# Wider TensorE groups for shared expert slots and for attention's values and sums

## The chip, the cores and the metric

The kernel runs on one NeuronCore of one Trainium2 chip. The metric is the device time of one execution in microseconds; the kernel before took 1078.47 us (median of three runs, 1077.15 to 1081.84).

## The reference

Three stages follow one another, all in float32:

- attention over 4 batches, 12 heads, 448 positions, head size 64, with capped scores: `scores = cap * tanh(q k^T / 8 / cap)`, softmax, times `v`;
- a feed-forward layer on the 1792 tokens of 768 numbers: `h = x @ w_in` (768 x 2048), `g = h * clip(h + 3, 0, 6) / 6`, `g @ w_out` (2048 x 768);
- a mixture of 8 experts: each token goes to the expert with the largest logit; `relu(x @ w1[e]) @ w2[e]` (768 x 1024 and 1024 x 768), scaled by the gate's probability and by a sigmoid.

```python
scores = cap * np.tanh(scale * np.matmul(q, k.transpose(0, 1, 3, 2)) / cap)
attn = np.exp(scores - scores.max(-1, keepdims=True))
x = np.matmul(attn / (attn.sum(-1, keepdims=True) + 1e-09), v)
for e in range(E):
    mask = e_idx == e
    out[mask] = gate_w[mask, None] * eom[mask, e, None] * (np.maximum(x[mask] @ w1[e], 0.0) @ w2[e])
```

## The kernel before, in words

All work is entered into one list of operations (`work.add`) with an engine, a due time in ns, an estimated duration, the operations it waits for and the buffers it uses. A planner (`Work.run`, L94) then walks through time by its own estimates and, on each engine, issues the ready operation with the earliest due time. The result is a fixed program order for each engine; on the chip an engine works through that order and waits where something isn't there yet. An operation with the engine `pe` may hold several matmuls; these stay together in TensorE's order, and matmuls of other operations come only between operations. The engine `sp` stands for SyncE, which issues the weight loads. For a load the planner counts 1400 ns, then the bytes at a fixed rate on one common line for all loads, then 1100 ns.

Buffers come in rings. A ring hands out its tiles in turn (`take`), and every operation that uses a tile waits for all operations on the tile's previous holder. The order of `take` in the program thus sets who gets a PSUM bank after whom.

**Attention** works on pairs of heads (`pair`, L505), six pairs to a batch. From the second batch on it lies between feed-forward work of the batch before. A pair's scores are four blocks of 112 keys: matmuls into S (L527), tanh (L536) and exp (L540) on ScalarE, with the exponentials `ee` kept in a ring of seven tiles, and VectorE's running sum `es` (L548). Then `pv(c0)` (L555) multiplies the exponentials of two blocks with the values, for two heads in two column halves of the array, into bank U, and `total()` (L562) adds `es` over the partitions into bank T with a matrix of ones. These are plain float32 matmuls, and each appears as two instructions in the profile. The loop at L567 makes two TensorE operations of it: `pv(0)`, waiting for the first two exponentials, and `(pv(2), total())`, waiting for the other two and for the sum. After that the sums are turned into reciprocals and multiplied in (L587 to L599).

**Feed-forward and expert products** are full-width matmuls on `float32r`: each float32 factor is split into a high and a low part and three matmuls (`mm3`, L605 to L608) add up one product.

**Expert slots.** A main slot takes 128 tokens of one expert (`first`, `second`, `h_T`, `x_T`); its matmuls are the L606 to L608 rows with `xTm` and `hTm`. Each product works through 6 or 8 chunks of 128 weight rows, and the products of all slots run in one fixed order: `first(i)`, `second(i-1)`, `first(i+1)` and so on. Each product needs its transposed left side, which goes through banks T and U in the order of program text.

Two **shared slots** (`quad_x`, `quad_h`, `quad_y`) take the remainders of several experts: 128 columns in parts of 64, 32 and 32, one expert for each part. `quad_product` (L1394) makes such a product, first with w1 (6 chunks, 2 x 512 columns), then with w2 (8 chunks, 2 x 384 columns). For each chunk t and each column half c there is a load of three conditional transfers, one for each part, into a buffer of the ring `QB` (two buffers cut from the tile `spare`), and one TensorE operation of four 32-column matmuls (L1416, eight instructions in the profile) that is due at `at + (2t+c) per` and ends that half's use of the buffer:

```python
x = work.add("sp", due - 14e3, 400, load, [qr] + gone, [hb], NQ * w * 512)
...
last[c] = work.add("pe", due, 40 + 1.75 * w, mm, [x, last[c]] + ready, [hd, accs[c], hb])
```

The shared slots are entered after main slots 2, 4, 7 and 9, 11, 13 (`QI`, L1445), so their transposes (L1433) stand in the order for T and U behind those of these slots. `spare` was the feed-forward's buffer before (`YT`, `ROWS`, `lt`); the shared slots may load into it once the last batch's rows are stored (`gone`).

Of the kernel before, what the change touches and what calls it, by code (L numbers as in the profile page):

```python
# [9 lines left out]
F32 = mybir.dt.float32  # L10
# [171 lines left out]
def attention_ffn_moe(  # L182
# [16 lines left out]
    B, H, S, D = q.shape  # L199
# [3 lines left out]
    C = 4  # L203
    P = S // C
    KD = DM // 128
    KF = DFF // 128
    KE = DE // 128
# [6 lines left out]
    NQ = len(PARTS)  # L214
# [14 lines left out]
    def pool(name, **kw):  # L229
        g = tc.tile_pool(name=name, reuse_waits="tile", **kw)  # L230
        return g, g.__enter__()

    def close(*gs):
# [18 lines left out]
        out=tri, in_=tri, pattern=[[1, P]], compare_op=ALU.is_gt, fill=0.0, base=0, channel_multiplier=-1  # L252
# [30 lines left out]
    g_fa, ffa = pool("ffa", bufs=1, side="left")  # L283
# [4 lines left out]
    def copier(out, in_):  # L288
        def fn(eng):
            if eng == "dve":  # L290
                nc.vector.tensor_copy(out=out, in_=in_)
            else:
                nc.scalar.activation(out=out, in_=in_, func=ACTF.Copy)  # L293

        return fn
# [7 lines left out]
    for nm in ("S0", "S1"):  # L303
        t = psp.tile([128, 2, 512], F32, name=nm)
# [22 lines left out]
    RR = ring(ffb, 2, [128, S], "r")  # L327
    GT = ring(ffb, HF, [128, 2, S], "gT", F32R)
    nspare = KD * S + C * RW + S
    spare = ffa.tile([128, max(nspare, 2 * NQ * 512 + KE * 128)], F32, name="spare")  # L330
    YT = Ring([spare[:, d * S:(d + 1) * S] for d in range(KD)])
    ROWS = Ring([spare[:P, KD * S:KD * S + C * RW]])
    lt = spare[:, nspare - S:nspare]
# [5 lines left out]
    work = Work()  # L339
# [5 lines left out]
    def t_head(g):  # L345
        return g * T0 / H if g < H else T0 + (g - H) * T1 / H
# [158 lines left out]
    def pair(n):  # L505
        b, p = divmod(n, H // 2)
        t0, per = t_head(2 * n), (t_head(2 * n + 2) - t_head(2 * n)) / 2
        hv, lv = loaded[n, "v2"]
        hw, ready = turned_qk[n]
        w = hw.t  # L510
# [3 lines left out]
        hu, hsum = UR.take(), ES.take()  # L514
        uv, es = hu.t, hsum.t
        many = 1 if b == 0 else 2
        et, last = [], None
        for c0 in range(0, C, many):
            at = t0 + c0 * per / 2
# [12 lines left out]
            for c, h in enumerate(hs):  # L532
                sv = h.t[:P, :, 0:S]
                x = work.add(
                    "act", at - 4e3 + c * 2e3, 900,
                    lambda sv=sv: A.activation(out=sv, in_=sv, func=ACTF.Tanh, scale=rcap[:P]), [s] + caps, [h])  # L536
                he = EE.take()
                x = work.add(
                    "act", at - 3e3 + c * 2e3, 900,
                    lambda sv=sv, he=he: A.activation(out=he.t, in_=sv, func=ACTF.Exp, scale=capt[:P]), [x], [h, he])  # L540
                et.append((he, x))
                k = len(et) - 1
                if k == 0:
                    continue
                one = et[0][0] if k == 1 else hsum
                last = work.add(
                    "dve", at - 2e3 + c * 2e3, 1002,
                    lambda he=he, one=one: V.tensor_tensor(out=es, in0=one.t, in1=he.t, op=ALU.add),  # L548
                    [et[0][1], x, last], [he, one, hsum] if k == 1 else [he, hsum])


        hd = TR.take()
        dv = hd.t

        def pv(c0):  # L555
            for c in range(c0, c0 + 2):
                for r in range(2):
                    nc.tensor.matmul(  # L558
                        out=uv[64 * r:64 * r + 64, 0:S], lhsT=by_head(hv)[:, r, c], rhs=et[c][0].t[:, r],
                        start=(c == 0), stop=(c == C - 1))  # L560

        def total():  # L562
            for r in range(2):
                nc.tensor.matmul(out=dv[64 * r:64 * r + 64, 0:S], lhsT=ones[:, 0:64], rhs=es[:, r], start=True, stop=True)  # L564

        x = None
        for c0 in range(0, C, 2):  # L567
            hes = [et[c][0] for c in (c0, c0 + 1)]
            if c0 + 2 < C:
                x = work.add(  # L570
                    "pe", t0 + c0 * per / 2, 1700, lambda: pv(0), [et[0][1], et[1][1], lv], [hu, hv] + hes, rows=P)
            else:
                x = work.add(
                    "pe", t0 + c0 * per / 2, 2450, lambda c0=c0: (pv(c0), total()), [x, et[2][1], et[3][1], last],
                    [hu, hv, hd, hsum] + hes, rows=P)
# [6 lines left out]
        def blocks(t):  # L582
            return t.rearrange("p (n w) -> p n w", w=32)

        at = min(t0 + 2.5 * per, T0 + b * T1 - 6e3 + p * 500)
        pe = x
        x = work.add("act", at, 467, lambda: A.activation(out=us, in_=dv[:, 0:S], func=ACTF.Copy), [pe], [hd, hy])  # L587
        x = work.add("dve", at, 535, lambda: V.transpose(out=blocks(rt), in_=blocks(us)), [x], [hy, hr])
        x = work.add("dve", at, 160, lambda: V.reciprocal(out=rc, in_=blocks(rt)[:, :, 0:1]), [x], [hr, hc])
        x = work.add(  # L590
            "dve", at, 535, lambda: V.transpose(out=blocks(us), in_=rc.to_broadcast([128, nb, 32])), [x], [hc, hy])
        x = work.add(
            "dve", at, 535, lambda: V.tensor_tensor(out=ux, in0=uv[:, 0:S], in1=us, op=ALU.mult), [x, pe], [hu, hx, hy])
        x = work.add(("dve", "act"), at, (302, 467), copier(x2[:, 0], ux), [x], [hx, xt])
        x = work.add(
            "dve", at, 535,
            lambda: V.tensor_tensor(out=x2[:, 1], in0=ux, in1=x2[:, 0].bitcast(F32), op=ALU.subtract),
            [x], [hx, xt])
# [126 lines left out]
    def chain(at, ops, fn, after, use=()):  # L725

        steps = [None]

        def some(n):
            if steps[0] is None:  # L730
                steps[0] = fn()
            for _ in range(n):
                next(steps[0])

        def rest(n):
            some(n)
            assert next(steps[0], None) is None

        for j, n in enumerate(ops):
            fn_ = rest if j == len(ops) - 1 else some  # L740
            after = [work.add("dve", at + j * 1.9e3, 200 * n - 130, lambda n=n, fn_=fn_: fn_(n), after, use)]
        return after[0]
# [483 lines left out]
    et = chain(te, (5, 5, 5, 2), early_table, [sw, placed[B - 2]])  # L1226
    er = work.add("sp", te + 3e3, 200, lambda: registers("e", NEARLY, "eei"), [et])
    he, x = lists("e", NEARLY, te + 4e3, [et, listed[B - 2]], TU)
# [133 lines left out]
    hd_, x = lists("d", NDYN, tm + SOON + 13e3, [ltab, listed[B - 1]], F)  # L1362
# [1 line left out]
    lr = work.add("sp", tm + SOON + 14e3, 1000, lambda: registers("d", NDYN, "dei"), [ltab])  # L1364


    QB = Ring([spare[:, j * NQ * 512:(j + 1) * NQ * 512].rearrange("p (q w) -> p q w", q=NQ) for j in range(2)])
    QT = Ring([spare[:, 2 * NQ * 512:2 * NQ * 512 + KE * 128].rearrange("p (t n) -> p t n", n=128)])
    quad = []

    def quad_regs():
# [6 lines left out]
    hq_, x = lists("q", NG, tm + SOON + 18e3, [qtab, listed[B - 1]], F)  # L1378
    qpg = small([128, NSH, NQ], "qpages")
    x = work.add(  # L1380
        "dve", tm + SOON + 18e3, 70,
        lambda: V.tensor_copy(out=qpg.rearrange("p s j -> p (s j)"), in_=hq_.t[:, 0:NG]), [x], [hq_])
# [6 lines left out]
    x = work.add("pe", tm + SOON + 18e3, 400, joined, [x], [hs_])  # L1389
    qlist = work.add("dve", tm + SOON + 18e3, 70, lambda: numbers("q", hs_, NSH), [x], [hs_])  # L1390
    qr = work.add("sp", tm + SOON + 22e3, 1600, quad_regs, [qtab])
    gone = [fin[B - 1, C - 1], listed[B - 1]]

    def quad_product(s, hd, ready, many, src, w, at, per):  # L1394
        accs = [F.take() for _ in range(2)]
        last = [None, None]
        for t in range(many):
            for c in range(2):
                hb = QB.take()
                due = at + (2 * t + c) * per  # L1400

                def load(t=t, c=c, hb=hb):
                    for j, (e, some) in enumerate(quad[s * NQ:(s + 1) * NQ]):
                        nc.sync.dma_start(
                            out=hb.t[:, j, 0:w],
                            in_=src[bass.ds(e, 1)].rearrange("o a b -> (o a) b")[
                                t * 128:(t + 1) * 128, c * w:(c + 1) * w],
                            cond=some > 0, bounds_check="skip_entire_dma")

                x = work.add("sp", due - 14e3, 400, load, [qr] + gone, [hb], NQ * w * 512)  # L1410

                def mm(t=t, c=c, hb=hb, acc=accs[c].t):
                    for j, (o, n) in enumerate(PARTS):
                        for a in range(o, o + n, QW):
                            part = slice(a, a + QW)
                            nc.tensor.matmul(  # L1416
                                out=acc[part, 0:w], lhsT=hd.t[:, t, part], rhs=hb.t[:, j, 0:w],
                                start=(t == 0), stop=(t == many - 1))

                last[c] = work.add("pe", due, 40 + 1.75 * w, mm, [x, last[c]] + ready, [hd, accs[c], hb])  # L1420
        return list(zip(accs, last))

    def quad_turned(src, after, n, at):
        hd = QT.take()
        hk = n // 2
# [77 lines left out]
    for i in range(NMAIN, NS):  # L1503
        with tc.If(used > slots[i][1]):
            work = Work()
# [39 lines left out]
```

## Time and profile before

| | us |
|---|---|
| median of 3 runs | 1078.47 |
| profiled execution | 1078.56 |
| span of its trace | 1076.8 |
| TensorE busy (matmul) | 1037.4 (96%) |
| VectorE busy | 729.5 (68%) |
| ScalarE busy | 663.1 (62%) |
| GpSimd busy | 94.8 (9%) |
| chain that ended last: TensorE | 77% of the span |
| chain that ended last: DMA | 4% of the span |

How to read it: the span runs from the first to the last instruction of the trace, and the execution's time has 1.76 us around it. Busy time of TensorE is modelled for overlapping matmuls, so a stretch of close starts counts as full. In timeline rows the first number is the start, the second the time to the end of the last instruction in the row, `xN` the number of instructions merged, and a bracket the idle time before the row and what ended it. Rows merge neighbours of the same kind, so a row `x16` of L1416 is two operations side by side.

### The profile page before, as it was taken

How to read it: one execution, taken by the hardware profiler on the slowest of the kernel's cores; microseconds unless marked ns; L12 is line 12 of the kernel's file. 1: busy time of each engine (PE TensorE's matmuls, PEld its weight loads, DVE VectorE, ACT ScalarE, POOL GpSimd, SP SyncE). 2: the span in 40 equal slices, each digit the busy share in tenths (PEclk: the TensorE clock that was granted, in tenths of full speed). 3: DMA queues.
4: the chain of work that ended last, by engine and by line, in shares of the span. 5: the costliest groups of instructions: out<-in, count | busy, mean ns of one | idle time of the engine just before them, and what ended most of it. 6: DMA issues, size and time to landing. Idle time of an engine off the chain costs nothing.

```text
span 1076.8 us, 17039 instructions
## 1 busy us (share of the span) xinstructions
PE 1037.4 (96%) x5764; PEld 792.6 (74%) x5764; DVE 729.5 (68%) x1155; ACT 663.1 (62%) x916; POOL 94.8 (9%) x122
## 2 busy tenths in 40 slices
PE   6979999999999999999999999999899999999996
PEld 4436777776777777677787899998677776877773
DVE  5999988965754665774465582627977777777762
ACT  5987677744754754564674352527566776776762
POOL 3211112100000000000000100000211111111001
PEclk9999999999999999999999999999999999999999
DMA  9889799862243343253232284462387689857455
GB/s 268 237 244 284 244 287 296 275 201 76 84 145 90 104 124 85 70 164 101 59 114 64 66 310 152 132 234 89 113 287 237 227 291 369 314 206 282 142 175 158
DMA packets 113997, 199.24 MB, mean 185 GB/s; under 512 B 43578, under 2 KB 68026, under 8 KB 113344
## 3 DMA queue, kind: packets, MB, share of 16 engines
q1 hardware_dynamic: 104304, 161.90, 46.7%
q0 software_dynamic: 9600, 36.19, 10.8%
q8 instruction: 47, 0.77, 0.3%
q14 instruction: 46, 0.38, 0.1%
HBM read 224.19 MB, written 25.76 MB: 232 GB/s over the span
## 4 chain that ended last, share of the span: by engine, by line
PE 77%; issue 9%; DVE 6%; DMA 4%; ACT 1%; POOL 0%; SPq 0%; POOLq 0%; DVEq 0%
PE F L606 14%; PE F L608 13%; PE F L607 13%; PE U L558 6%; PE S L606 6%; PE S L527 5%; PE S L607 5%; PE S L608 5%; PE F L1416 2%; DMA out_dram<-y,tkd 2%; DMA spare<-in_moe_w_dram 2%; PE T L564 1%; DVE ring L1270 1%; PE T L489 1%; DVE es L548 1%
## 5 line engine op out<-in xcount | busy, mean ns | idle before, releaser
L635 DVE TENSOR_TENSOR ws<-wr,ws 128x768 fp32r<-128x768 f32 (+1 forms) x112 | 119.6, 1068 | 77.5 <-ACT ws L632 75.1
L632 ACT ACTIVATE ws<-wr 128x768 fp32r<-128x768 f32 (+1 forms) x112 | 104.6, 934 | 42.6 <-PE F L607 27.8
L606 PE MATMUL F<-gT,ws 128*128 128x448 f32 x320 | 121.5, 380 | 0.0
L608 PE MATMUL F<-gT,ws 128*128 128x448 f32 x320 | 117.0, 366 | 0.0
L607 PE MATMUL F<-gT,ws 128*128 128x448 f32 x320 | 116.9, 365 | 0.0
L536 ACT ACTIVATE S<-S,rcap 112x896 f32<-112x896 f32 x96 | 91.1, 980 | 24.2 <-PE S L527 23.8
L540 ACT ACTIVATE ee<-S,capt 112x896 f32<-112x896 f32 x96 | 93.3, 1016 | 0.2
L527 PE MATMUL S<-qk 64*112 64x448 f32 x576 | 76.6, 390 | 12.0 <-ACT qk L495 5.1
L606 PE MATMUL S<-ring,hTm 128*128 128x384 f32 x224 | 82.8, 370 | 0.0
L659 ACT ACTIVATE r<-F,three 128x448 f32<-128x448 f32 x64 | 40.7, 636 | 63.3 <-PE F L608 62.6
L607 PE MATMUL S<-ring,hTm 128*128 128x384 f32 x224 | 75.7, 338 | 1.4 <-DVE ring L1270 1.4
L527 PEld LDWEIGHTS S<-qk 64*112 64x112 f32 x576 | 47.2, 175 | 40.3 <-issue 13.6
L606 PEld LDWEIGHTS F<-gT,ws 128*128 128x128 f32 x320 | 60.1, 188 | 22.3 <-issue 18.2
L608 PE MATMUL S<-ring,hTm 128*128 128x384 f32 x224 | 75.7, 338 | 0.2 <-DVE hTm L1298 0.2
L606 PE MATMUL F<-xTa,ws 128*128 128x448 f32 x192 | 73.8, 384 | 1.6 <-ACT spare L293 0.9
L606 PE MATMUL F<-xTb,ws 128*128 128x448 f32 x192 | 73.7, 384 | 1.6 <-ACT spare L293 0.9
L558 PE MATMUL U<-ee,v 112*64 112x448 f32 x336 | 73.8, 561 | 0.0
L1270 DVE TENSOR_TENSOR ring<-w2B,ring 128x768 fp32r<-128x768 f32 x56 | 53.1, 958 | 30.2 <-ACT ring L1266 29.5
L607 PE MATMUL F<-xTb,ws 128*128 128x448 f32 x192 | 70.3, 366 | 0.0
L608 PE MATMUL F<-xTb,ws 128*128 128x448 f32 x192 | 70.2, 366 | 0.0
L1270 DVE TENSOR_TENSOR ring<-w2A,ring 128x768 fp32r<-128x768 f32 x56 | 53.0, 956 | 25.1 <-ACT ring L1266 21.8
L608 PE MATMUL F<-xTa,ws 128*128 128x448 f32 x192 | 69.8, 364 | 0.0
(291 smaller groups left out, 2287.3 us busy)
## 6 DMA issues: line engine op xcount, KB each, us to landing
wr<-wsi SPq DMA_DIRECT2D x64, 384.0 KB
wr<-wso SPq DMA_DIRECT2D x48, 512.0 KB
w1A<-in_moe_w_dram SPq DMA_DIRECT2D x42, 512.0 KB
w2A<-in_moe_w_dram SPq DMA_DIRECT2D x56, 384.0 KB
w1B<-in_moe_w_dram SPq DMA_DIRECT2D x42, 512.0 KB
w2B<-in_moe_w_dram SPq DMA_DIRECT2D x56, 384.0 KB
spare<-in_moe_w_dram SPq DMA_DIRECT2D x72, 256.0 KB
spare<-in_moe_w_dram SPq DMA_DIRECT2D x96, 192.0 KB
```

The source lines that it names most:

```text
L527: nc.tensor.matmul(out=h.t[:P, r, 0:S], lhsT=w[o, 1, i, (c0 + c) * P:(c0 + c + 1) * P], rhs=w[o, 0, j], start=(t == 0), stop=(t == 2))
L536: lambda sv=sv: A.activation(out=sv, in_=sv, func=ACTF.Tanh, scale=rcap[:P]), [s] + caps, [h])
L540: lambda sv=sv, he=he: A.activation(out=he.t, in_=sv, func=ACTF.Exp, scale=capt[:P]), [x], [h, he])
L558: nc.tensor.matmul(out=uv[64 * r:64 * r + 64, 0:S], lhsT=by_head(hv)[:, r, c], rhs=et[c][0].t[:, r], start=(c == 0), stop=(c == C - 1))
L606: nc.tensor.matmul(out=acc, lhsT=lh, rhs=rh, start=first, stop=False)
L607: nc.tensor.matmul(out=acc, lhsT=lh, rhs=rl, start=False, stop=False)
L608: nc.tensor.matmul(out=acc, lhsT=ll, rhs=rh, start=False, stop=last)
L632: lambda: A.activation(out=s[:, 0, 0:n], in_=t, func=ACTF.Copy), [x], [hw, hs])
L635: lambda: V.tensor_tensor(out=s[:, 1, 0:n], in0=t, in1=s[:, 0, 0:n].bitcast(F32), op=ALU.subtract),
L659: "act", t1, 518, lambda: A.activation(out=r, in_=acc, func=ACTF.Relu, bias=three), [last], [ha, hr])
L1270: lambda: V.tensor_tensor(out=hs.t[:, 1, 0:w], in0=raw(), in1=hs.t[:, 0, 0:w].bitcast(F32), op=ALU.subtract),
L1416: nc.tensor.matmul(out=acc[part, 0:w], lhsT=hd.t[:, t, part], rhs=hb.t[:, j, 0:w], start=(t == 0), stop=(t == many - 1))
```

## The change

Two edits and what they need. In `pair`, batches from the second on get one TensorE operation that holds `pv(0)`, `pv(2)` and `total()`; it waits for all four exponentials, the sum and the values, and is due when the second operation was due. The first batch keeps the two. In `quad_product` a chunk's two loads are entered first, and then one TensorE operation computes both column halves; it waits for both loads and is due when the first half was due. `QB` has three buffers in place of two, and `QT` moves behind them. `spare` is as long as the larger of two terms: the feed-forward's 6212 columns, and the shared slots' need, now 6080, which was 4096.

```diff
-    spare = ffa.tile([128, max(nspare, 2 * NQ * 512 + KE * 128)], F32, name="spare")
+    spare = ffa.tile([128, max(nspare, 3 * NQ * 512 + KE * 128 + S)], F32, name="spare")
...
-        for c0 in range(0, C, 2):
+        if b > 0:
+            x = work.add(
+                "pe", t0 + per, 4150, lambda: (pv(0), pv(2), total()), [e[1] for e in et] + [last, lv],
+                [hu, hv, hd, hsum] + [e[0] for e in et], rows=P)
+        for c0 in range(0, C, 2) if b == 0 else ():
...
-    QB = Ring([... for j in range(2)])
-    QT = Ring([spare[:, 2 * NQ * 512:2 * NQ * 512 + KE * 128]...])
+    QB = Ring([... for j in range(3)])
+    QT = Ring([spare[:, 3 * NQ * 512:3 * NQ * 512 + KE * 128]...])
...
-        last = [None, None]
+        last = None
         for t in range(many):
+            due = at + 2 * t * per
+            bufs, ready_w = [], []
             for c in range(2):
                 hb = QB.take()
-                due = at + (2 * t + c) * per
...
-                x = work.add("sp", due - 14e3, 400, load, [qr] + gone, [hb], NQ * w * 512)
-
-                def mm(t=t, c=c, hb=hb, acc=accs[c].t):
+                bufs.append(hb)
+                ready_w.append(work.add("sp", due + c * per - 14e3, 400, load, [qr] + gone, [hb], NQ * w * 512))
+
+            def mm(t=t, bufs=bufs):
+                for c in range(2):
                     for j, (o, n) in enumerate(PARTS):
                         for a in range(o, o + n, QW):
                             part = slice(a, a + QW)
                             nc.tensor.matmul(
-                                out=acc[part, 0:w], lhsT=hd.t[:, t, part], rhs=hb.t[:, j, 0:w],
+                                out=accs[c].t[part, 0:w], lhsT=hd.t[:, t, part], rhs=bufs[c].t[:, j, 0:w],
                                 start=(t == 0), stop=(t == many - 1))
 
-                last[c] = work.add("pe", due, 40 + 1.75 * w, mm, [x, last[c]] + ready, [hd, accs[c], hb])
-        return list(zip(accs, last))
+            last = work.add("pe", due, 200 + 3.1 * w, mm, ready_w + [last] + ready, [hd] + accs + bufs)
+        return [(a, last) for a in accs]
```

## Rows read from the trace of the kernel before

**Rows 1.** The page's first part: busy us (share of the span) xinstructions.

```profile
PE 1037.4 (96%) x5764; PEld 792.6 (74%) x5764; DVE 729.5 (68%) x1155; ACT 663.1 (62%) x916; POOL 94.8 (9%) x122
```

**Rows 2.** Windows: stretch, length, busy us per engine, clock, DMA share, GB/s.

```profile
85.00:605.00 520.00, 514.28 (x2756) 398.79 (x2755) 350.92 (x583) 313.13 (x439) 30.88 (x50) 1.00 0.49 148
...
790.00:955.00 165.00, 162.96 (x932) 122.24 (x931) 120.30 (x131) 118.36 (x157) 21.71 (x17) 1.00 0.81 283
```

**Rows 3.** Timeline of TensorE around a lone `pv(0)`: start, us, instruction.

```profile
307.97 0.36 PE L607 MATMUL F<-gT,ws 128*128 128x448 f32 x1
308.17 0.37 PE L608 MATMUL F<-gT,ws 128*128 128x448 f32 x1
308.46 1.73 PE L558 MATMUL U<-ee,v 112*64 112x448 f32 x8
...
310.43 0.36 PE L607 MATMUL F<-gT,ws 128*128 128x448 f32 x1
```

**Rows 4.** Timeline of TensorE: a second half with its sums, the next scores.

```profile
267.02 1.72 PE L558 MATMUL U<-ee,v 112*64 112x448 f32 x8
268.57 0.92 PE L564 MATMUL T<-es,ones 112*64 112x448 f32 x4
...
272.06 1.48 PE L527 MATMUL S<-qk 64*112 64x448 f32 x12
```

**Rows 5.** Timeline of TensorE around one 512-column half of a shared chunk.

```profile
817.25 0.40 PE L607 MATMUL S<-ring,xTm 128*128 128x512 f32 x1
817.48 0.39 PE L608 MATMUL S<-ring,xTm 128*128 128x512 f32 x1
817.80 1.06 PE L1416 MATMUL F<-spare 128*32 128x512 f32 x8
...
819.13 0.40 PE L607 MATMUL S<-ring,xTm 128*128 128x512 f32 x1
```

**Rows 6.** Timeline of TensorE around two neighbouring halves, first shared slot's start.

```profile
793.66 0.40 PE L608 MATMUL S<-ring,xTm 128*128 128x512 f32 x1
793.99 1.92 PE L1416 MATMUL F<-spare 128*32 128x512 f32 x16
...
796.18 0.40 PE L607 MATMUL S<-ring,xTm 128*128 128x512 f32 x1
```

**Rows 7.** Timeline of TensorE around one 384-column half.

```profile
1046.64 0.34 PE L607 MATMUL S<-ring,hTm 128*128 128x384 f32 x1
1046.81 0.34 PE L608 MATMUL S<-ring,hTm 128*128 128x384 f32 x1
1047.08 0.85 PE L1416 MATMUL F<-spare 128*32 128x384 f32 x8
...
1048.15 0.33 PE L607 MATMUL S<-ring,hTm 128*128 128x384 f32 x1
```

**Rows 8.** A piece of the chain, a timeline row, and L1416's waits (us, times).

```profile
795.08 8.56 DMA spare<-in_moe_w_dram
...
803.69 2.40 PE L1416 MATMUL F<-spare 128*32 128x512 f32 x8 [1.30 <-DMA spare<-in_moe_w_dram]
...
  DMA spare<-in_moe_w_dram: 15.5, 24
```

**Rows 9.** Timeline of TensorE: shared slot's transposes, next slot's, its first product.

```profile
854.65 0.60 PE L1433 MATMUL T<-ident,h 128*128 128x128 f32 x4
...
858.60 0.49 PE L1285 MATMUL T<-ident,xrow 128*128 128x128 f32 x3
...
864.14 0.48 PE L606 MATMUL S<-ring,xTm 128*128 128x512 f32 x1
```

**Rows 10.** Timeline of TensorE: second shared slot's start, and the end.

```profile
957.59 1.92 PE L1416 MATMUL F<-spare 128*32 128x512 f32 x16
...
1066.13 0.34 PE L608 MATMUL S<-ring,hTm 128*128 128x384 f32 x1
...
1067.66 2.41 PE L1416 MATMUL F<-spare 128*32 128x384 f32 x8 [0.41 <-DMA spare<-in_moe_w_dram]
```

More of the change, by code (lines that the diff above doesn't have):

```diff
@@ L1364, in attention_ffn_moe @@
     lr = work.add("sp", tm + SOON + 14e3, 1000, lambda: registers("d", NDYN, "dei"), [ltab])
-    QB = Ring([spare[:, j * NQ * 512:(j + 1) * NQ * 512].rearrange("p (q w) -> p q w", q=NQ) for j in range(2)])
-    QT = Ring([spare[:, 2 * NQ * 512:2 * NQ * 512 + KE * 128].rearrange("p (t n) -> p t n", n=128)])
+    QB = Ring([spare[:, j * NQ * 512:(j + 1) * NQ * 512].rearrange("p (q w) -> p q w", q=NQ) for j in range(3)])
+    QT = Ring([spare[:, 3 * NQ * 512:3 * NQ * 512 + KE * 128].rearrange("p (t n) -> p t n", n=128)])
     quad = []
```

## The prediction

> **What bounds the kernel now.** I read the busy shares first: TensorE is busy for 1037.4 of 1076.8 us, and no other engine passes 730 [rows 1]. Then the windows by stage: from 85 to 605 us (attention of later batches beside the feed-forward) TensorE is busy for 514.3 of 520, from 790 to 955 (first shared slot) for 163.0 of 165 [rows 2]. Busy alone would not prove a bound, so third came the timeline of TensorE: consecutive full matmuls start one ordinary spacing apart, 0.20 us for 448 columns [rows 3], 0.23 for 512 [rows 5], 0.17 for 384 [rows 7]. So time taken off TensorE comes off the end, unless something else is late. Fourth, the places where TensorE does stand still beside shared-slot groups: 24 waits for `spare` loads, 15.5 us on its two halves together [rows 8], part of it covered. Fifth, the tail: the last main matmul starts at 1066.13 and the last shared group at 1067.66, taking 2.41 us [rows 10]. Main work and shared slots therefore finish nearly together, and a change has to shorten both.
>
> **Values and sums in one group (L566 to L575).** No instruction is added or removed; per pair of heads one return to full-width matmuls disappears. Standing alone, `pv(0)` costs, from the matmul before it to the second after it, 310.43 - 308.17 = 2.26 us, less two ordinary spacings of 0.205: 1.85 us [rows 3]. The same eight instructions with `total` behind them take 268.57 - 267.02 = 1.55 us [rows 4]. One boundary is 0.30 us. There are 18 pairs from the second batch on; at 16 the early half stands between full-width matmuls on at least its left and is followed by them or by scores, at two (near 279 and 456 us) transposes follow it, and I count these two as one. 17 x 0.30 = 5.1 us. It lies on the bounding engine, so it goes through.
>
> The early values now wait for all four exponentials and for the sums, as the second half did before, so the end of the group has no new condition. Behind the group in TensorE's order stand feed-forward matmuls and the next pair's scores; they would pay if the planner put it too early, but it enters the order only when planned ready. The four `ee` tiles are held longer, out of seven, so the next pair's fourth exponential may wait on ACT, with the weight copies behind it. I cost this at nothing: the next scores came 2.6 us after a finished group (269.49 by the row, then 272.06) [rows 4], so the old tiles are free before new ones are wanted. If that cover were gone, ACT would be late by one such group, 2.4 us per pair at worst; earlier free use of bank U could give back one 0.30 more. Ends for this edit: 10 us gained, 18 x 2.4 = 43 lost; the lost end needs every pair to collide, and I take 5.1 gained.
>
> **Both halves of a shared chunk in one group (L1394 to L1421).** A single 512-column half costs 819.13 - 817.48 = 1.65, less two spacings of 0.235: 1.18 us [rows 5]. The trace already holds what the new form will look like: at the start of each shared slot both halves happened to be neighbours, and 16 instructions cost 796.18 - 793.66 = 2.52, less 0.47: 2.05 us [rows 6]. Saving 2 x 1.18 - 2.05 = 0.31 per pair. For 384 columns a half costs 1048.15 - 1046.81 = 1.34 less 0.34: 1.00 us [rows 7]; the second half inside a group is 2.05 - 1.18 = 0.87 at 512 columns, so 0.65 at 384, and the saving is 0.35. Two slots have 6 + 8 pairs each. Of the 12 wide pairs two are neighbours already, of the 16 narrow ones the last one (at the tail): 10 x 0.31 + 15 x 0.35 = 8.4 us. Together 13.5 us of TensorE's time.
>
> **Three buffers and the new wait.** The region keeps its size (the other term of the maximum, 6212 columns, still exceeds 6080), the 168 conditional transfers and their bytes stay, and so does SP's due time of each. What changes is when a buffer comes free. Before, two halves in two buffers alternated, and each load ran while the other half was waited for and used. Now a pair needs two of three buffers: one half of the next pair can be there early, the second can only be issued when the pair is done. The wait sits on TensorE with all main matmuls behind it; a load on SP that waits for the pair has main weight loads behind it. Price of a late load from the trace: a load issued at 795.08 ended a wait 8.56 us later, TensorE idled 1.30 us and the group took 2.40 us where 1.06 is usual [rows 5, 8], since its three transfers came piecewise. I take about 9 us of the 15.5 as uncovered, an estimate: of the shown one 1.30 is idle and 1.34 lies inside the group. They could all go (a half is loaded ahead, the first such wait falls) or as much again could come; nearest is the row itself, one wait for one load per cycle as before, so I take zero, ends -9 and +9.
>
> For the pace of a slot two things oppose each other. Within a load-bound cycle the second half's 0.87 us no longer lies beside a load: 14 x 0.87 = 12 us later at worst. On the other hand the group is due at the first half's due time, and the last group of either phase no longer trails it by half a cycle: in slot 1, 793.99 to the transposes at 854.65 is 60.7 us [rows 6, 9] for six pairs, some 10 us per pair, so up to 5 us earlier in each of two phases. I take zero, between -10 and +12.
>
> **Sum.** The main stream loses 13.5 us. The second shared slot begins after a fixed main step (the transposes of slot 9), at 957.59 [rows 10]; ahead of that lie 5.1 us and half of 8.4: it starts 9.3 us earlier. Its own 112.5 us to the last matmul (957.59 to 1070.07) I leave as they are, since loads pace them, not TensorE. So the slot's end, not the main stream, sets the end: -9.3 us, and the remaining 4.2 turn into waits before the last groups. The profiled execution took 1078.56 us (span 1076.8 and 1.76 around it), 0.09 above the median of 1078.47. 1078.56 - 9.3 = 1069.3, say 1069.
>
> **Rivals.**
> *Loads never gate.* Then the slot's end follows the main stream, 1078.5 - 13.5 = 1065, and down to 1056 if all 9 us of stalls go too. For it: three buffers, and a pair's first half early. Against it: 24 waits stand in the trace with loads that had whole half cycles of time.
> In a sentence apart: the Trainium skill (DMA: Bandwidth & Descriptors, its fit of a fixed 2 us plus bytes over 436 GB/s) would put a 768 KB half at some 3.8 us, an estimate, which is well inside a cycle, so by it this rival would be the likeliest case; the trace shows 8.56 us for one [rows 8], so it speaks for the rule only where the queue is empty.
>
> *The pair's loads stretch the first phase.* The transposes after it share banks T and U with the next slot's: 854.65, then 858.60, and that slot's first product at 864.14 [rows 9]. Main products run in a fixed order, so a later first phase stops TensorE nearly one for one. Six pairs fit in the old time up to a period of (60.7 - 2.05)/5 = 11.7 us. With a load of 8.56, the piecewise excess of 1.3 and a 2.05 us group the period is 11.9; with one main block of six 0.20 us spacings queued ahead of it, 13.1, and 5 x 1.4 = 7 us are lost in one slot. If it hits one slot the sum is -13.5 + 7, and with the slower second phase (8 x 0.65 = 5) about -1.5: 1077, no change.
>
> *Slower.* The same place, both slots, at a period of 14.2 us: 2 x 5 x 2.5 = 25 lost against 13.5, +11.5: 1090. It decides from a period of about 13.6 (19 us lost, +0.5%). For it: DMA is at its busiest here, 283 GB/s over the first slot [rows 2]. Against it: the group is due earlier, and 10 us was the period with the loads as they are.
>
> *It doesn't do what it says:* the second half's transfers land piecewise inside the group, which then costs two singles. That returns the 8.4 us and leaves 5.1: 1073.
>
> **How the numbers follow.** I give 0.44 to the forecast (its own range 1065 to 1073), 0.27 to loads that never gate, 0.06 to the torn group (1073, split between faster and same), 0.14 to the stretched phase, 0.09 to slower. A difference of 0.5%, 5.4 us, is about what a measurement here tells from no change, so faster means below 1073.1. Of the forecast 0.43 lies below that, of the torn group 0.04: faster 0.74, same 0.17, slower 0.09. The range reaches from 1060 (half of the stalls gone beside the full saving) to 1080 (the stretched phase with a little more).
>
> **What will show it.** In attention from the second batch on, blocks of 16 instructions of L558 followed by the sums, some 0.30 us less per pair, and each batch from 255 us on shorter by about 1.8. In the shared slots 28 blocks of 16 at about 1.85 us and 1.4 us, and the second slot's first block about 9 us earlier. The quantity that decides is the wait ahead of these blocks: unchanged in sum, I am right; gone, 1065; 2 us or more per block, or idle time ahead of the next slot's first product, no gain. The forecast is also wrong if the last main matmul and the last shared group still end together (then the slot followed the main stream), or if scores or exponentials start waiting for `ee`.

## The result

The changed kernel takes 1067.77 us (median of five runs, 1065.96 to 1069.59) against 1078.47 us before: a ratio of 0.9898 with a 95% interval of 0.9877 to 0.9918, that is 10.7 us or 1.0% faster. 1069 had been forecast. The profiled execution took 1065.96 us, with a span of 1064.2 us, 12.6 us shorter than before.

### The profile after

The busy shares, which answer to [rows 1]: TensorE's instructions are the same in number, and its busy time is 12.9 us less, about all that the span lost.

```profile
PE 1024.5 (96%) x5764; PEld 799.7 (75%) x5764; DVE 725.5 (68%) x1154; ACT 661.0 (62%) x917; POOL 93.6 (9%) x122
```

TensorE's timeline around one attention group, then one wide and one narrow shared group of the changed kernel (start, us, instruction; L558 and L564 keep their numbers, L606 to L608 are now L610 to L612, L1416 is L1423):

```profile
504.03 0.36 PE L612 MATMUL F<-gT,ws 128*128 128x448 f32 x1
504.32 3.23 PE L558 MATMUL U<-ee,v 112*64 112x448 f32 x16
507.38 0.92 PE L564 MATMUL T<-es,ones 112*64 112x448 f32 x4
...
814.62 0.39 PE L612 MATMUL S<-ring,xTm 128*128 128x512 f32 x1
814.94 1.92 PE L1423 MATMUL F<-spare 128*32 128x512 f32 x16
...
817.13 0.40 PE L611 MATMUL S<-ring,xTm 128*128 128x512 f32 x1
...
1039.63 0.34 PE L612 MATMUL S<-ring,hTm 128*128 128x384 f32 x1
1039.90 1.50 PE L1423 MATMUL F<-spare 128*32 128x384 f32 x16
1041.33 0.45 PE L610 MATMUL S<-ring,hTm 128*128 128x384 f32 x1
1041.61 0.34 PE L611 MATMUL S<-ring,hTm 128*128 128x384 f32 x1
```

Both parts of the grouping are there, near the forecast price. The sixteen instructions of the values take 507.38 - 504.32 = 3.06 us where the two halves cost 1.85 + 1.55 [rows 3, 4]: 0.34 saved. A wide pair costs 817.13 - 814.62 = 2.51, less two spacings of 0.235: 2.04 us, against 2 x 1.18 [rows 5]; a narrow pair 1.98 - 0.34 = 1.64 against 2 x 1.00 [rows 7]: 0.32 and 0.36 saved. Before, L1416 stood in 53 uninterrupted blocks; L1423 stands in 28, 25 fewer.

The waits of L1423 for its loads (us in total, times), counted over TensorE's weight loads and matmuls together, answer to the last line of [rows 8] and have become fewer:

```profile
  DMA spare<-in_moe_w_dram: 11.4, 15
```

The second shared slot of the changed kernel and its end on TensorE answer to [rows 10]. Below them stand the last scatters to the output, which GpSimd issues (`tkd`: a main slot's results, `tkq`: a shared slot's): the last one before the change, then the last two after it.

```profile
950.70 1.92 PE L1423 MATMUL F<-spare 128*32 128x512 f32 x16
...
1052.96 1.50 PE L1423 MATMUL F<-spare 128*32 128x384 f32 x16
...
1056.40 0.34 PE L612 MATMUL S<-ring,hTm 128*128 128x384 f32 x1
```

```profile
1072.65 0.97 POOL L1131 DMA_INDIRECT out_dram<-y,tkq  x1 [3.14 <-ACTq L1504]
```

```profile
1056.24 0.97 POOL L1135 DMA_INDIRECT out_dram<-y,tkq  x1 [11.09 <-issue]
1059.79 0.97 POOL L1135 DMA_INDIRECT out_dram<-y,tkd  x1 [2.58 <-DMA out_dram<-y,tkq]
```

The slot starts 6.9 us earlier than before and ends 1070.07 - 1054.46 = 15.6 us earlier; the main stream's last matmul starts 9.7 us earlier and is now the later of the two. The order at the end has turned round: the last scatter of main results waits 2.58 us for the slot's scatter, which used to be last.

### The profile page after: what moved, and what is told of

Same layout as the page of the kernel before. It is cut to its first block, busy times and chain, and to the rows that moved or that the text cites. A ratio compares the mean times of both kernels' runs of the same rounds, so it can differ in the third digit from the quotient of the medians.

```text
span 1064.2 us, 17020 instructions
## 1 busy us (share of the span) xinstructions
PE 1024.5 (96%) x5764; PEld 799.7 (75%) x5764; DVE 725.5 (68%) x1154; ACT 661.0 (62%) x917; POOL 93.6 (9%) x122
## 4 chain that ended last, share of the span: by engine, by line
PE 70%; DVE 14%; issue 10%; DMA 3%; ACT 2%; POOL 0%; SPq 0%; POOLq 0%; DVEq 0%; ACTq 0%
PE F L610 12%; PE F L612 11%; PE F L611 11%; PE S L610 6%; PE S L611 6%; PE S L612 6%; PE U L558 5%; PE S L527 5%; PE F L1423 2%; DVE es L548 2%; DMA out_dram<-y,tkd 2%; DVE cva L408 1%; DVE cva L411 1%; DVE ring L1274 1%; DVE ws L639 1%
## 5 line engine op out<-in xcount | busy, mean ns | idle before, releaser
L610 PE MATMUL F<-gT,ws 128*128 128x448 f32 x320 | 120.1, 375 | 1.6 <-ACT xTb L293 1.0
L612 PE MATMUL F<-gT,ws 128*128 128x448 f32 x320 | 117.0, 366 | 0.0
L610 PE MATMUL S<-ring,hTm 128*128 128x384 f32 x224 | 81.9, 366 | 0.0
L612 PE MATMUL S<-ring,hTm 128*128 128x384 f32 x224 | 76.3, 341 | 0.0
L610 PE MATMUL F<-xTa,ws 128*128 128x448 f32 x192 | 73.7, 384 | 0.8 <-DVE lg L780 0.6
L610 PE MATMUL F<-xTb,ws 128*128 128x448 f32 x192 | 73.6, 383 | 0.9 <-DVE lg L780 0.6
L610 PEld LDWEIGHTS F<-gT,ws 128*128 128x128 f32 x320 | 60.1, 188 | 16.0 <-issue 8.7
L612 PE MATMUL F<-xTb,ws 128*128 128x448 f32 x192 | 70.2, 366 | 0.0
L558 PE MATMUL U<-ee,v 112*64 112x448 f32 x336 | 70.0, 556 | 0.0
L612 PE MATMUL F<-xTa,ws 128*128 128x448 f32 x192 | 69.8, 364 | 0.0
L611 PE MATMUL F<-xTa,ws 128*128 128x448 f32 x192 | 69.5, 362 | 0.0
```

Source lines behind the costliest of these rows:

```text
L558: nc.tensor.matmul(out=uv[64 * r:64 * r + 64, 0:S], lhsT=by_head(hv)[:, r, c], rhs=et[c][0].t[:, r], start=(c == 0), stop=(c == C - 1))
L610: nc.tensor.matmul(out=acc, lhsT=lh, rhs=rh, start=first, stop=False)
L611: nc.tensor.matmul(out=acc, lhsT=lh, rhs=rl, start=False, stop=False)
L612: nc.tensor.matmul(out=acc, lhsT=ll, rhs=rh, start=False, stop=last)
```

## The experiments

Every run was timed against the kernel before on the same chip, in five rounds. E1 to E4 shared a chip, E5 to E7 another, E8 a third, and the changed kernel was timed earlier; across these groups the ratio is the safer comparison. Single runs of one kernel spread by up to 8 us (the kernel before: 1074.92 to 1083.02), so medians are given beside ratios. A stage below is the stretch from one batch's router matmuls to the next batch's. In the profiles, stage lengths after the first 256 us repeat far better than the totals: the fourth batch's stage took 172.82 to 172.85 us in all four profiles with the old attention there.

| kernel | median, us | ratio to before (95%) |
|---|---|---|
| attention edit only (E1) | 1080.18 | 1.0018 (1.0003 to 1.0034) |
| shared-slot edit only (E2) | 1069.22 | 0.9916 (0.9897 to 0.9935) |
| the change with two buffers (E3) | 1073.43 | 0.9952 (0.9936 to 0.9968) |
| three buffers only (E4) | 1072.27 | 0.9938 (0.9923 to 0.9954) |
| the change, attention from the third batch (E5) | 1068.70 | 0.9895 (0.9873 to 0.9917) |
| E2 and the second batch's attention (E6) | 1072.70 | 0.9937 (0.9916 to 0.9959) |
| E2 and attention in three groups (E7) | 1078.81 | 0.9990 (0.9975 to 1.0006) |
| the change, second slot earlier (E8) | 1066.77 | 0.9887 (0.9868 to 0.9906) |

The third batch's stage repeats as well once TensorE's granted clock is read beside it (1.00 is the full clock; less means that part of the stage ran at the lower of its two levels). Windows of that stage: before, changed kernel, E4 (old attention), E1 (grouped); the clock is the third column from the end.

```profile
255.68:433.06 177.38, 174.52 (x941) 134.55 (x940) 102.98 (x168) 101.05 (x140) 0.00 (x0) 1.00 0.35 103
256.44:432.00 175.56, 172.81 (x942) 135.39 (x941) 102.39 (x166) 101.73 (x143) 0.00 (x0) 1.00 0.34 104
255.66:434.16 178.50, 175.91 (x941) 135.73 (x941) 103.17 (x168) 101.30 (x140) 0.00 (x0) 0.99 0.34 102
257.57:434.13 176.56, 174.08 (x942) 136.88 (x940) 102.45 (x166) 101.80 (x143) 0.00 (x0) 0.99 0.34 103
```

At equal clock the grouping takes 1.8 to 1.9 us off this stage.

**E1, attention only.** The kernel before with the `if b > 0` group of the diff.

> Only the attention edit, on the kernel before: from the second batch on both halves and the sums in one group. Theory A (each removed boundary on TensorE is 0.30 to 0.34 us and goes through to the end): 17 to 18 boundaries, 5.1 to 6.1 us less, 1072.4 to 1073.4. Rival B (the boundary is gained but half of it comes back as other waits of TensorE in attention, as the changed kernel's matmuls suggest, which stood only 2.3 us earlier at 605 us): 2 to 3.5 us less, 1075 to 1076.5. Rival C (the edit gives nothing, the shared slots give all): 1078.

No gain at all, rather 2 us lost. A and B fall for this kernel by its median; C comes nearest. Its profile shows a gain all the same: the third and fourth batches' stages took 176.56 (at clock 0.99) and 171.76 us, against 177.38 (at 1.00) and 172.84. But its twelve runs fall into two groups of six, 1077.0 to 1079.4 and 1081.0 to 1082.8 us. The profiled run (1077.55) is of the first group, so what made the second is not shown.

**E2, shared slots only.** The change without that group.

> Only the shared-slot edit: both halves in one group, three buffers; attention as before. Theory A (25 boundaries of 0.31 to 0.35 us, nothing else): 8.4 us less, 1070. Rival B (the slot also runs at a quicker pace and its waits fall, so it gives more than its boundaries): 10 us or more less, 1068 or below. Rival C (second slot sets the end and gains only half): 4 us less, 1074.

8.9 us less: the shared slots make nearly all of the gain. The size lies between A and B and doesn't decide between them. E4 does, since A left no gain to anything but the boundaries.

**E3, two buffers under the grouping.**

```diff
-    QB = Ring([... for j in range(3)])
+    QB = Ring([... for j in range(2)])
```

> The changed kernel with two buffers in place of three, so that no half of the next pair can be loaded before the pair is done. Theory A (the third buffer is what keeps the pace; pairs without it wait for two loads one after the other, 28 pairs, some 2 us longer each, which delays the next slot's transposes and the end): 8 to 25 us slower than the changed kernel, 1076 to 1093. Rival B (loads are quick enough for a whole pair, the grouping alone makes the gain): within 2 us of the changed kernel, 1066 to 1070.

5.7 us slower than the changed kernel by the medians (0.9952 against 0.9898), less than A gave and more than B. It is still 4.7 us faster than the kernel before on the same chip. The third buffer is needed for the rest, and the profile says where: TensorE's timeline of E3 at its end.

```profile
1050.58 0.34 PE L612 MATMUL S<-ring,hTm 128*128 128x384 f32 x1
1051.46 4.53 PE L1423 MATMUL F<-spare 128*32 128x384 f32 x16 [0.54 <-DMA spare<-in_moe_w_dram]
1057.11 2.57 PE L1423 MATMUL F<-spare 128*32 128x384 f32 x12 [1.13 <-DMA spare<-in_moe_w_dram]
1060.22 2.04 PE L1423 MATMUL F<-spare 128*32 128x384 f32 x8 [0.54 <-DMA spare<-in_moe_w_dram]
1062.47 1.83 PE L1423 MATMUL F<-spare 128*32 128x384 f32 x8 [0.21 <-DMA spare<-in_moe_w_dram]
1064.73 1.39 PE L1423 MATMUL F<-spare 128*32 128x384 f32 x4 [0.43 <-SPq L1511]
```

The main stream is done at 1050.9 us, earlier than in any other kernel here. After that nothing is left but 48 instructions of the slot, three pairs, 4.3 us of work at the 1.43 us from a narrow pair's start to the next matmul in the changed kernel. They take 15 us. What SyncE did meanwhile, its waits from 1048 us on (us in total, times, longest) and its transfers:

```profile
SPq L1409 <- PE F L1423: 5.0, 2, 4.7
1049.05 13.09 SPq L1409 DMA_DIRECT2D spare<-in_moe_w_dram  x18
```

SyncE stood 4.7 us until the pair ahead began to free its buffers, and then issued the 18 transfers of the three pairs nearly without a pause, one in some 0.73 us, so 4.4 us for a pair of 1.43 us. The wait for a buffer is what the forecast had feared for three buffers: it is real, and with two it starts the late end. After it the rate of issuing sets nearly all of the pace: TensorE takes up the first part 2.4 us after its transfer's issue (1051.46) and the last 3.5 us after (1061.80, 1065.28).

**E4, three buffers, nothing grouped.** Only the `QB`, `QT` and `spare` lines of the diff.

> The kernel before with three buffers in place of two, nothing grouped. Theory A (the gain is boundaries, a buffer alone removes none; it can remove at most the waits for loads, about 9 us, most of it hidden behind the main stream's own order): 0 to 3 us less, 1075.5 to 1078.5. Rival B (the second slot's pace sets the end, and the buffer alone quickens it): 5 us or more less, 1073 or below.

5.8 us less; rival B. The last slot group of E4 on TensorE ends at 1056.75, while the main stream goes on to its last matmul at 1063.91:

```profile
1055.44 1.31 PE L1416 MATMUL F<-spare 128*32 128x384 f32 x8
```

```profile
1063.91 0.34 PE L608 MATMUL S<-ring,hTm 128*128 128x384 f32 x1
```

Before, the slot ended 3.6 us behind the main stream [rows 10]. One more buffer took 13.3 us off the slot's end and 2.2 off the main stream's, and the slot no longer sets the end. So more than half of the gain had nothing to do with boundaries. The slot took 99.7 us here (957.10 to 1056.75), against 112.5 before and 113.0 in E3 (953.08 to 1066.12), where the pairs are grouped but share two buffers: it is the buffer that shortens the slot. SyncE's waits until L1416 or L1423 freed a buffer, both slots together (us in total, times, longest), say the same: before, E4, the changed kernel, E3.

```profile
SPq L1404 <- PE F L1416: 45.4, 38, 7.3
SPq L1404 <- PE F L1416: 29.4, 23, 8.5
SPq L1409 <- PE F L1423: 26.2, 25, 4.4
SPq L1409 <- PE F L1423: 46.2, 34, 4.7
```

From E4 to E2 the grouping of pairs adds 3 us by medians. In the two profiles the first slot starts at the same time (795.24 and 795.22 us), and the main stream ends 4.4 us earlier with the grouping (1064.25 and 1059.81), against 22 boundaries fewer (50 blocks and 28), worth 7.3 us. Most of the difference can be found: E2 has one wait of a main slot's transposes for VectorE, 2.0 us, that E4 doesn't have, and by the starts of its matmuls it stands about 1.2 us longer in and before the slot's groups.

```profile
PE T L1285 <- DVE xTm L1298: 2.0, 1, 2.0
```

**E5 and E6, which batch's attention.** The condition `b > 0` of the changed kernel becomes `b > 1` in E5 and `b == 1` in E6.

> The changed kernel, but attention grouped only from the third batch on (12 pairs; the second batch keeps its two groups). The profiles so far: the third and fourth batches' stages lose 1.8 and 1.1 us by the grouping, the second batch's stage nothing (it loses 2.5 us of boundaries and finds 1.2 to 2.9 us of idle waits of TensorE). Theory A (the second batch's grouping is worth nothing or costs): 0.5 to 2 us less than the changed kernel, 2 to 3 us less than with the shared-slot edit alone, ratio to before 0.987 to 0.989. Rival B (every pair's boundary is worth the same): 2 us more than the changed kernel, ratio 0.991.

> The shared-slot edit, and attention grouped in the second batch alone (6 pairs). Theory A: no gain over the shared-slot edit alone (ratio to before 0.9916) or a loss up to 2 us, ratio 0.9915 to 0.9935, and new idle waits of TensorE for VectorE and ScalarE between 85 and 256 us. Rival B (six boundaries of 0.33 us go through): 2 us less, ratio 0.990.

E5 is not to be told from the changed kernel, and lies between its two theories. E6 is 0.0021 worse than E2, 2.3 us: B's 0.990 lies outside its interval, while A's loss can't be told from none, since the intervals of E6 and E2 overlap. Its profile names what is late in the second batch: TensorE's waits of E6 from 84 to 259 us (us in total, times, longest).

```profile
PE F L610 <- DVE r L666: 2.6, 4, 1.4
PE F L610 <- ACT xTb L293: 1.1, 1, 1.1
PE F L610 <- ACT us L591: 0.8, 1, 0.8
```

In E2 the same stretch has one wait, 1.0 us. VectorE is busy there for 150.2 of 175 us (E2), with the conversion of the weights beside the splitting, so a quicker TensorE soon waits for it. Over nine profiles TensorE is idle in this stage for 0 to 1.0 us with the old attention there (before, E2, E4, E5) and for 1.4 to 3.9 us with the grouped one (changed kernel, E1, E3, E6, E8). The stage took 174.68 us in E6 and 172.23 in E2. But with the changed kernel at 170.91 and E5, old attention there, at 170.44, the stage varies by itself by as much; no gain in it is shown, and the loss is likely rather than settled.

**E7, one boundary more per pair.** On E2, `pv(2)` and `total()` become two operations, the second due 1.5 us later, from the second batch on.

> The shared-slot edit, and attention cut the other way from the second batch on: the early values, the late values and the sums are three groups with other work between (one boundary more per pair, 18 in all). Theory A (a boundary is 0.33 us of TensorE and comes through where TensorE is dense, that is in the third and fourth batch): 12 to 18 x 0.33 = 4 to 6 us slower than the shared-slot edit alone, ratio to before 0.995 to 0.9975. Rival B (what the grouping gained and lost in attention is the order of the waits, not the boundary): within 2 us of it, ratio 0.990 to 0.9935.

9.6 us slower than E2 by the medians, 8.0 by the ratios: A's sign, and more than its size. The windows of the third and the fourth batch's stage: E2, then E7.

```profile
256.39:433.86 177.47, 174.61 (x941) 134.42 (x940) 102.95 (x168) 101.13 (x140) 0.00 (x0) 1.00 0.33 103
433.86:606.70 172.84, 169.97 (x913) 132.31 (x912) 100.53 (x164) 97.15 (x135) 3.10 (x16) 1.00 0.30 95
261.34:440.75 179.41, 177.18 (x942) 133.39 (x941) 103.47 (x168) 100.67 (x140) 0.00 (x0) 1.00 0.33 102
440.75:615.38 174.63, 172.01 (x914) 131.43 (x913) 100.49 (x165) 96.26 (x134) 3.10 (x16) 1.00 0.30 94
```

Each stage has six groups more than in E2. Both stages are longer, the third batch's by 179.41 - 177.47 us, the fourth's by 174.63 - 172.84, all at clock 1.00: 1.9 and 1.8 us, 0.30 to 0.32 for each added boundary, which thus comes through in full. The second's is 2.3 us longer (174.50 against 172.23 from its first feed-forward matmul), but that stage varies by as much by itself. Most of the rest, 2.7 us, arose before the second batch's stage (it begins at 86.84 against 84.16 us), in the first batch's attention, whose code is the same in both; why is open.

**E8, the second shared slot one main slot earlier.** On the changed kernel, `QI` has (8, 10, 13) for (9, 11, 13) and `QA` 7.2 for 8.2.

> The changed kernel with the second shared slot entered one main slot earlier. In the changed kernel the slot's last group ends only 2.3 us before the main stream, and the last scatter of main results then waits 2.58 us for the slot's scatter. Theory A (the main stream sets the end now, and this wait is all that the slot still costs at the tail): the wait goes, 2 to 3 us less than the changed kernel, ratio to before 0.987 to 0.988, the last main matmul where it was. Rival B (the slot's loads then collide with the main slots' loads, which the late start avoided): TensorE waits more, ratio 0.990 or above. Rival C (the slot still sets the end): 5 us or more less than the changed kernel.

GpSimd's end in E8, with main's last matmul at 1062.44 us:

```profile
1053.50 0.97 POOL L1135 DMA_INDIRECT out_dram<-y,tkq  x1 [20.75 <-ACT y L1481]
1058.28 1.06 POOL L1135 DMA_INDIRECT out_dram<-y,tkd  x1 [3.81 <-ACT ring L1270]
1064.04 0.97 POOL L1135 DMA_INDIRECT out_dram<-y,tkd  x1 [4.70 <-ACTq L1511]
```

The wait between the last two scatters is gone: the last one starts 1.6 us after the start of the last matmul, 3.4 us in the changed kernel. That is 1.8 us, and 1.0 us by the medians. So A's wait went, at less than A's size; whether E8 beats the changed kernel these runs can't tell (0.9887 and 0.9898). The profiled run is the slowest of E8's six (1071.01 us), so its total is not compared. C falls: the slot's end has no more to give.

## Why the prediction was right, and where it was not

The time came within 1.2 us of the forecast, the direction and the range held. The price of a boundary held within 0.04 us: 0.30, 0.31 and 0.35 us forecast, 0.34, 0.32 and 0.36 found. Removing six or adding six in the third batch's stage gives 0.30 to 0.32 each.

That the total fits is luck. By medians the 10.7 us are 5.8 from the third buffer (E4), 3 from the shared grouping beside it (E4 to E2), and what is left, under 2, from attention. (Taken in the other order, the buffer gives 5.7, E3.) The forecast had nothing from the buffer, 4.2 from the shared grouping and 5.1 from attention: one term too small and one too large. Nor does the number choose between the forecast's 1069 and the 1065 of the loads that never gate; 1067.77 lies between them.

**The step that failed** is "I take zero" for the three buffers, and with it "Its own 112.5 us to the last matmul (957.59 to 1070.07) I leave as they are". It was argued from one wait for one load per cycle before and after. In the changed kernel the slot takes 1054.46 - 950.70 = 103.8 us, 8.7 less, inside the bounds given (10 gained to 12 lost), but not zero; E4 shows 5.8 us of gain from the buffer alone. What was missed: the slot of before had no slack at all. Its pace, not TensorE, put its last group behind the main stream, and with one buffer more that pace rose: 99.7 us in E4. SyncE's waits for a free buffer fell with it, from 45.4 to 29.4 us. That this happens because a half lies ready while the next load runs is my reading; no run here takes the load times themselves apart.

**The conclusion from it failed with it.** "The slot's end, not the main stream, sets the end" was the case before and is the case with two buffers (E3). In the changed kernel the main stream is last, by 2.3 us, near to what the forecast had named as its refutation (both ending together). The waits that were to decide neither stayed nor went: 15.5 us in 24 became 11.4 in 15. The rival of loads that never gate came nearer in which stream ends last, though not in its reason.

**Attention was put at 5.1 us** and gave 2 us at most: E1 shows 2 us lost, the change over E2 2 us gained by ratios whose intervals overlap, and together they don't settle its sign in the total. By stages it can be followed. The third batch's stage gains 1.8 to 1.9 us at equal clock, six boundaries at the forecast price, as the forecast had said ("each batch from 255 us on shorter by about 1.8"). The profiles of E5 and E8, where that stage's clock was 0.98, show 177.81 and 177.86 us and hide the gain. The fourth batch's stage gains 0.9 to 1.3 us (171.55 to 171.91 against 172.82 to 172.85). It holds only five of the early halves, since the early half of a batch's first pair fell before the router's matmuls, and transposes follow one of the five; that accounts for a part, and the rest of the difference from the third stage stays open. Idle time doesn't explain it: TensorE is idle there for 2.9 us before and after. The second batch's stage shows no gain:

```profile
84.69:255.68 170.99, 170.99 (x910) 132.70 (x908) 148.61 (x254) 115.23 (x164) 27.77 (x34) 1.00 0.81 249
85.53:256.44 170.91, 169.54 (x914) 133.83 (x912) 145.88 (x251) 115.52 (x165) 27.11 (x33) 1.00 0.79 246
```

Before, TensorE is busy for all of it; in the changed kernel it is busy for 1.4 us less and idle for 1.4 us. So "it lies on the bounding engine, so it goes through" failed in the second batch. The term counted 17 boundaries as if TensorE were the only bound in all three stages. [rows 2] gave one line for all of them; a window on the second batch alone would have shown VectorE busy for 148.6 of 171.0 us, against 103.0 of 177.4 in the third.

In the two profiles the forecast's 9.3 us, meant as 5.1 from attention and 4.2 from the first slot, came as 1.5 us by the first slot's start (793.99 to 792.45), and 5.4 more by the second's. From there the main stream gained another 2.8 (its last matmul 9.7 earlier), and the tail 2.9, as the slot no longer ended last: 12.6 in all.

**The rivals of a stretched first phase** and of a slower kernel are refuted. The first slot's wide pairs stand at 792.45, 802.48, 814.94, 825.99, 837.23 and 848.30 us, a period of 11.2, under the 11.7 at which it would have begun to cost; its transposes (before: [rows 9]) come 59.9 us after its start, 0.8 less than before, and main's next product starts 3.6 us earlier. The changed kernel's TensorE there:

```profile
852.35 0.60 PE L1440 MATMUL T<-ident,h 128*128 128x128 f32 x4
...
860.50 0.48 PE L610 MATMUL S<-ring,xTm 128*128 128x512 f32 x1
```

The group was not torn either: 24 of the 28 blocks ran without a break in their starts.

## What to carry to other kernels

Where small column-tiled matmuls are strewn among full-width ones, count the returns and price one from the starts around it; grouping pays that price only where no second engine soon holds TensorE up. Before grouping work that shares buffers, look which of two interleaved streams ends last and what its pace is made of: a buffer more can be worth as much as all the boundaries. When two profiles of one stage differ by a microsecond, read the granted clock of both before explaining it. And a change that moves time from one stream to the other should be priced at the end of both.

## What the runs showed of the hardware

A change between column-tiled and full-width matmuls costs TensorE 0.30 to 0.36 us in and out, whichever the tile (64 or 32 columns). It is not the plain float32 that costs: a float32 transpose in full width between the same matmuls doesn't show the price. In the changed kernel it starts 0.17 us after the matmul before it, the ordinary spacing, while a shared group starts 0.27 us after (1039.63, 1039.90). From that matmul to the second one behind the three transposes it is 0.68 us; less two spacings that is 0.34, or 0.11 for each transpose, and the transposes start 0.11 us apart.

```profile
828.83 0.34 PE L612 MATMUL S<-ring,hTm 128*128 128x384 f32 x1
829.00 0.49 PE L1289 MATMUL T<-ident,xrow 128*128 128x128 f32 x3
829.25 0.43 PE L610 MATMUL S<-ring,hTm 128*128 128x384 f32 x1
829.51 0.33 PE L611 MATMUL S<-ring,hTm 128*128 128x384 f32 x1
```

The Trainium skill (TensorEngine Tiling (Array Packing), Key Properties) says that changing the tiling mode drains TensorE, and that changing only the tile does not. The trace agrees: inside a shared group the matmuls on its different column tiles start within 0.03 us of one another, and the price is paid per group, not per matmul.

TensorE's granted clock differed between profiles of the same stage. In the third batch's stage with the old attention, 1.00 went with 177.38 to 177.47 us (before, E2, E6) and 0.99 with 178.50 (E4); with the grouped one, 1.00 went with 175.56, 0.99 with 176.56 and 176.66 (E1, E3), and 0.98 with 177.81 and 177.86 (E5, E8). With either form, 0.99 in place of 1.00 cost 1.0 to 1.1 us. It fell behind the idle time at the router, but not always: from 260 to 264 us TensorE was busy for 2.31 of 4 us in E4 and for 2.43 in E2, and only E4 was granted less from 264 to 268.

```profile
264.00:268.00 4.00, 4.00 (x15) 3.23 (x13) 3.71 (x9) 0.95 (x2) 0.00 (x0) 0.57 0.63 156
264.00:268.00 4.00, 3.60 (x18) 2.72 (x20) 3.72 (x11) 1.67 (x4) 0.00 (x0) 1.00 0.55 158
```
